# Rounds of seven products in a fused attention and expert kernel: the order of copies, leaky steps, weight splits and decodes

## The chip, the cores and the metric

One core of a Trainium2 chip runs the whole program. The metric is the device time of one execution in microseconds (us), lower is better. Engines are named as the profile names them: PE is TensorE (PEld its weight loads), DVE is VectorE, ACT is ScalarE, POOL is GpSimd, SP is SyncE, which here issues the weight loads. Each engine works through its own queue in order, and a step that waits holds up all that stands behind it in that queue.

## The reference

Causal attention over 2 x 12 heads of 448 positions and 64 dims gives a matrix x of 896 tokens by 768. Two expert layers follow:

```python
h = x @ w_in                      # 768 -> 2048, the part that this change is about
g = np.maximum(0.01 * h, h)       # "leaky"
x = g @ w_out                     # 2048 -> 768
xn = x / rms(x) * rms_g
y = (silu(xn @ w_gate) * (xn @ w_val)) @ w_out2
```

The inputs arrive as 64-bit floats in HBM, the output is 32-bit.

## The kernel before, in words

**Stages.** Attention takes the first 92 us of the profiled execution, `x @ w_in` the stretch from 92 to 204 us, `g @ w_out` runs to 325 us, the gated layer and the last product fill the rest. All matrix work is done with each 32-bit operand split in a high part and a low part, so a product of one 128-row block of weights takes three matmuls: high by high, low by high, high by low.

**Decoding a piece of weights** (`decode`, L96 to L145). A piece n is 128 x 768 values of 64 bits. Its steps are: `load` (SP issues the transfer into one of two `raw` buffers), `rebias` on ACT (L112, writes tile `we`, called e(n) here), `last` on DVE (L119, `ws`), `shift` on DVE (L123) and `sign` on DVE (L127), which finish e(n), then `high` on ACT (L134) and `low` on DVE (L140), which split e(n). `begin(n)` does the load, `word(n)` does rebias to sign, `act(n)` the high and `dve(n)` the low part. The tile `we` has two buffers, so e(n) takes the place of e(n-2), and rebias(n) waits until e(n-2) was read for the last time.

**Straight blocks.** The 2048 outputs are 16 blocks of 128. Blocks 0 to 7 are computed plainly: `block(f)` is 36 matmuls on piece f, and `leaky` on ACT (L214) writes the result to its place. Between them the operand x is prepared for what comes later: `whole_x(c)` (DVE, L601), `xsums(c)` (DVE, L605 to L608), `xsplit(c, 0)` (two copies on ACT, L565) and `xsplit(c, 1)` (two subtractions on DVE, L148), for c of 0, 1, 2.

**Rounds of seven products.** Blocks 8 to 15 are taken in pairs, n of 4 to 7 (blocks f = 2n and f + 1), by Winograd's form of Strassen's scheme: seven products of 9 matmuls each in place of eight. The weights of a round are the quarters a11, a12 (from e(2n)) and a21, a22 (from e(2n+1)). `combine(n)` makes their four sums on POOL (L587) into the tiles `suma` and `sumb`. `plain(n)` splits a11 and a12 (products 1 and 2), `corner(n)` splits a22 (product 4, tiles `hid` and `lod`), `sums(n, 0)` splits `suma` (products 6 and 7), `sums(n, 1)` splits `sumb` (products 5 and 3, tiles `hie` and `loe`). Each split is a copy on ACT (L565) and a subtraction on DVE (L148).

**Order in a round** on PE: 6, 7, 5, then 1 of the next round, 3, 2 of the next round, 4. Products 1, 6, 5 and 3 add to one PSUM bank, one after the other, and each partial sum has to be copied out by ACT (`held`, L627) before the next product adds to the bank: call these copies t1 (after 1), u2 (after 6) and u4 (after 5). Products 7 and 4 share a second bank, and 2 has a third. `join` (DVE, L631) adds a kept copy and a bank, `bend` (ACT, L214) is leaky on a joined block. So product 5 waits for u2, product 3 for u4, the next round's product 6 for t1, and product 4 for the join that reads the second bank. Before, the queue of ACT in a round is: copies of `plain(n+1)`, `bend(f-1, 0)`, copy of `corner(n+1)`, u2, u4, copy of `sums(n+1, 0)`, t1, rebias(f+4), `bend(f+1, 1)`, rebias(f+5), copy of `sums(n+1, 1)`, `leaky(f, 1)`, `bend(f+2, 0)`.

**What sets the order.** Up to the end of the rounds the instructions stand on each engine as the text writes them (`manual_schedule`, L544). From L795 on a planner in the framework orders them by what is ready, and it can move them forward: the first steps of the next stage, `turn_in` (L799 to L804: a copy on ACT, L802, and a subtraction on DVE, L148, that split a block of g), run in the trace among the steps of the last round. In the next stage the first matmuls need `turn_in` of the first blocks and the split pieces 16 and 17.

Of the kernel before, what the change touches and what calls it, by code (L numbers as in the profile page):

```python
# [15 lines left out]
P = 128  # L16
# [58 lines left out]
def fused_kernel(tc, q, k, v, w_in, w_out, w_gate, w_val, w_out2, rms_g, out):  # L75
# [3 lines left out]
    with ExitStack() as top:  # L79
# [13 lines left out]

        xT = [slot(f"a{i}") for i in range(KC)]

        def decode(src, n, m, hi=None, lo=None):  # L96


            N = n * m
            L = {}  # L100

            def load(_=None):
                raw = wst.tile([P, N], I64, tag="raw", name="raw")
                SP.dma_start(out=raw.rearrange("p (n m) -> p n m", m=m), in_=src)
                L["w"] = raw.bitcast(I32).rearrange("p (n t) -> p n t", t=2)

            def rebias(eng="A"):

                e = L["e"] = wst.tile([P, N], I32, tag="we", name="we")[:]
                out, src = e.bitcast(F32), L["w"][:, :, 1].bitcast(F32)  # L110
                if eng == "A":
                    ACT.activation(out=out, in_=src, func=AF.Copy, scale=2.0 ** -112)  # L112
                else:
                    POOL.tensor_scalar(out=out, in0=src, scalar1=2.0 ** -112, scalar2=1.0, op0=ALU.mult, op1=ALU.mult)

            def last(_=None):

                s = L["s"] = wst.tile([P, N], I32, tag="ws", name="ws", bufs=1)[:]
                DVE.tensor_scalar(out=s, in0=L["w"][:, :, 0].bitcast(U32), scalar1=2.0 ** -29, scalar2=7.0,  # L119
                                  op0=ALU.mult, op1=ALU.min)  # L120

            def shift(_=None):
                DVE.scalar_tensor_tensor(out=L["e"], in0=L["e"], scalar=3, in1=L["s"],  # L123
                                         op0=ALU.logical_shift_left, op1=ALU.bitwise_or)

            def sign(_=None):
                DVE.scalar_tensor_tensor(out=L["e"], in0=L["w"][:, :, 1], scalar=-0x80000000, in1=L["e"],  # L127
                                         op0=ALU.bitwise_and, op1=ALU.bitwise_or)

            def high(eng="A"):  # L130
                L["hi"] = wst.tile([P, N], F32R, tag="hi", name="hi") if hi is None else hi
                L["lo"] = wst.tile([P, N], F32R, tag="lo", name="lo") if lo is None else lo
                if eng == "A":
                    ACT.copy(out=L["hi"], in_=L["e"].bitcast(F32))  # L134
                else:
                    POOL.tensor_scalar(out=L["hi"], in0=L["e"].bitcast(F32), scalar1=1.0, scalar2=1.0,
                                       op0=ALU.mult, op1=ALU.mult)

            def low(_=None):
                DVE.tensor_tensor(out=L["lo"], in0=L["e"].bitcast(F32), in1=L["hi"].bitcast(F32), op=ALU.subtract)  # L140

            def parts():
                return [(L["hi"][:, i * m:(i + 1) * m], L["lo"][:, i * m:(i + 1) * m]) for i in range(n)]

            return [load, rebias, last, shift, sign, high, low], parts, L  # L145
# [398 lines left out]
        with tc.manual_schedule(), tc.tile_pool(name="w1", bufs=1) as w1:  # L544
            enc, steps_of, aw, xs, ub, parts_at = {}, {}, {}, {}, {}, {}

            def begin(n):
                src, k_, m_, _ = pieces[n]
                steps_of[n], parts_at[n], enc[n] = decode(src, k_, m_)
                steps_of[n][0]()  # L550

            def run(n, lo, hi):
# [6 lines left out]
            def place(pool, tag, n, bufs=None):  # L559
                kw = {} if bufs is None else dict(bufs=bufs)  # L560
                return [pool.tile([P, n], F32R, tag=t, name=t, **kw) for t in ("hi" + tag, "lo" + tag)]

            def split(pair, x, what=2):
                if what != 1:
                    ACT.copy(out=pair[0], in_=x)  # L565
                if what:
                    rest(pair[1], x, pair[0])

            def e(n, j):
                return enc[2 * n + j]["e"].bitcast(F32)  # L570

            def plain(n):
                pair = place(wst, "", 2 * THIRD)
                split(pair, e(n, 0))
                aw[n, 1], aw[n, 2] = halves(*pair)

            def corner(n):
                aw[n, 4] = place(w1, "d", THIRD, 2)
                split(aw[n, 4], e(n, 1)[:, THIRD:])

            def combine(n):
# [21 lines left out]
            def xsums(c):  # L603
                x = xs[c]
                DVE.tensor_tensor(out=x[:, 0].rearrange("p (b s) -> p b s", b=B), in0=x[:, :, S:],  # L605
                                  in1=x[:, 0].rearrange("p (b s) -> p b s", b=B), op=ALU.subtract)
                DVE.tensor_tensor(out=x[:, 1, S:], in0=x[:, 1, S:], in1=x[:, 0, :S], op=ALU.subtract)
                DVE.tensor_tensor(out=x[:, 1, :S], in0=x[:, 1, :S], in1=x[:, 1, S:], op=ALU.subtract)  # L608

            def xsplit(c, what):  # L610
                for i in (1, 0):
                    t = xs[c, i] = slot(SUMS[c][i]) if what == 0 else xs[c, i]
                    split((t[:, 0], t[:, 1]), xs[c][:, i], what)
                    for b, m in enumerate(((5, 7), (4, 6))[i]):
                        xs[c, "p", m] = cols(t, b)
                xs[c, "p", 1], xs[c, "p", 2], xs[c, "p", 3] = cols(xT[c], 0), cols(xT[c + 3], 0), cols(xT[c + 3], 1)
# [16 lines left out]
            def bend(f, b):  # L633
                leaky(f, b, kept(f, b))
# [21 lines left out]
            def word(n):  # L656
                run(n, 1, 5)

            def bent(f, pss):
                for b in range(B):  # L660
                    leaky(f, b, pss[b])
# [20 lines left out]
            dve(3)  # L682
            leaky(1, 1, ps)
            xsplit(0, 1)
            xsums(1)
            xsplit(1, 0)
            word(4)
            begin(5)
            pss = block(2)
            act(4)  # L690
            xsplit(1, 1)
            dve(4)
            bent(2, pss)
            word(5)
            begin(6)
            pss = block(3)
            act(5)
            whole_x(2)
            dve(5)
            bent(3, pss)  # L700
            xsums(2)
            xsplit(2, 0)
            word(6)
# [17 lines left out]
            combine(4)  # L721
            pss = block(6)
            plain(4)
            corner(4)
            bent(6, pss)
            sums(4, 1)
            pss = block(7)
            sums(4, 0)
            bent(7, pss)
            gF.append(slot(HOME[4], F32))  # L730
            word(10)
# [3 lines left out]
            begin(13)  # L735
            two(4)
            join(8, 0, ub[4, 1], ub[4, "b"])
            bend(8, 0)
            combine(5)
            for n in range(4, LAST + 1):  # L740
                more = n < LAST
                f = 2 * n
                if more:
                    plain(n + 1)
                    if n > 4:
                        bend(f - 1, 0)
                    corner(n + 1)
                else:
                    bend(f - 1, 0)
                times(n, 6, ub[n], start=False)  # L750
                u2 = held(mx, "t0", ub[n])
                v_ = bank()
                times(n, 7, v_)
                times(n, 5, ub[n], start=False)
                u4 = held(mx, "t2", ub[n])
                join(f + 1, 1, u4, v_)
                if more:
                    sums(n + 1, 0)
                    one_(n + 1)
                    word(f + 4)  # L760
                    if f + 6 < NF1 + 2:
                        begin(f + 6)
                    bend(f + 1, 1)
                    run(f + 5, 1, 2)
                else:
                    two(n)
                    bend(f + 1, 1)
                    act(NF1)
                    dve(NF1)
                times(n, 3, ub[n], start=False)  # L770
                if more:
                    sums(n + 1, 1)
                leaky(f, 1, ub[n])
                if more:
                    run(f + 5, 2, 5)
                    if f + 7 < NF1 + 2:
                        begin(f + 7)
                    gF.append(slot(HOME[n + 1], F32))
                else:
                    act(NF1 + 1)  # L780
                    dve(NF1 + 1)
                if n + 1 < LAST:
                    two(n + 1)
                    join(f + 2, 0, ub[n + 1, 1], ub[n + 1, "b"])
                    bend(f + 2, 0)
                elif not more:
                    join(f, 0, ub[n, 1], ub[n, "b"])
                    bend(f, 0)
                if n + 2 <= LAST:
                    combine(n + 2)  # L790
                times(n, 4, v_, start=False)
                join(f + 1, 0, u2, v_)
# [157 lines left out]
```

## Time and profile before

| what | value |
|---|---|
| runs, us | 591.24, 591.34 (median), 591.89 |
| the profiled execution's own time, us | 589.87 |
| its span, first to last instruction, us | 588.1 |
| granted TensorE clock, mean | 1.00 of full speed |
| PE busy | 576.2 us, 98% of the span, 3246 matmuls |
| DVE, ACT, POOL busy | 417.8, 282.0, 75.9 us |
| transfers | 65.02 MB, mean 111 GB/s |

PE's busy share is near its end, so what can be saved without removing matmuls is PE's idle time. Idle time of another engine counts only where PE ends up waiting for it. The profiled execution was 1.47 us (0.25%) shorter than the median of the three runs.

### The profile page before, as it was taken

The numbers are of one execution on the slowest core, as the hardware profiler recorded it, in microseconds if no ns is written. First come the engines' busy times: TensorE is split into PE (matmuls) and PEld (weight loads), VectorE is DVE, ScalarE is ACT, GpSimd is POOL, SyncE is SP. The second block draws the span as 40 slices with busy tenths as digits, with TensorE's granted clock in tenths as the row PEclk, the third lists the DMA queues.
The fourth block names the chain that finished last, engine by engine and source line by source line (L and its number), as shares of the span: only waits on it lengthen the run. The fifth ranks groups of instructions, "written<-read, shape, count | busy, mean of one in ns | idle before, by whom it ended". The sixth has DMA issues, their size and how long they took to land.

```text
span 588.1 us, 8475 instructions
## 1 busy us (share of the span) xinstructions
PE 576.2 (98%) x3246; PEld 520.1 (88%) x3246; DVE 417.8 (71%) x728; ACT 282.0 (48%) x537; POOL 75.9 (13%) x137
## 2 busy tenths in 40 slices
PE   9999999999799999999999999999999999999997
PEld 6687778889688899999999999999999999999997
DVE  6989878886777895765755998797797796840000
ACT  6999984344555682432334743443443444420000
POOL 6666650003333000000000000000000000000000
PEclk9999999999999999999999999999999999999999
DMA  8974403135333323253234244343343351721001
GB/s 182 204 188 81 131 1 108 53 109 161 108 107 108 107 72 107 91 177 110 90 107 124 94 159 152 116 153 116 108 159 111 108 159 56 192 76 41 27 28 40
DMA packets 83351, 65.02 MB, mean 111 GB/s; under 512 B 35440, under 2 KB 80240, under 8 KB 83312
## 3 DMA queue, kind: packets, MB, share of 16 engines
q1 hardware_dynamic: 82352, 64.27, 37.3%
q8 instruction: 25, 0.41, 0.3%
q10 hardware_dynamic: 960, 0.23, 0.2%
q14 instruction: 14, 0.11, 0.1%
HBM read 61.74 MB, written 2.75 MB: 110 GB/s over the span
## 4 chain that ended last, share of the span: by engine, by line
PE 82%; issue 10%; ACT 4%; DVE 3%; POOL 1%; POOLq 0%; ACTq 0%; DVEq 0%
PE mm L154 10%; PE mm L155 10%; PE mm L153 10%; PE mm L824 7%; PE mm L823 7%; PE mm L822 7%; PE mm L907 5%; PE mm L905 5%; PE mm L906 5%; PE pt L386 4%; PE x L408 3%; PE mm L623 3%; PE s L347 3%; PE qk L292 2%; ACT we L112 1%
## 5 line engine op out<-in xcount | busy, mean ns | idle before, releaser
L154 PE MATMUL mm<-a,lo 128*128 128x448 f32 x324 | 118.5, 366 | 0.8 <-DVE lo L140 0.8
L153 PE MATMUL mm<-a,hi 128*128 128x448 f32 x324 | 118.5, 366 | 0.0
L155 PE MATMUL mm<-a,hi 128*128 128x448 f32 x324 | 118.3, 365 | 0.0
L123 DVE SCALAR_TENSOR_TENSOR we<-we,ws 128x768 int32<-128x768 int32 (+1 forms) x70 | 65.5, 936 | 29.0 <-ACT we L112 27.5
L134 ACT CAST hi<-we 128x768 fp32r<-128x768 f32 (+1 forms) x51 | 41.4, 812 | 87.4 <-PE mm L823 38.9
L112 ACT ACTIVATE we<-raw 128x768 f32<-128x768 f32 (+1 forms) x68 | 60.3, 889 | 36.1 <-DVE lo L140 19.2
L140 DVE TENSOR_TENSOR lo<-we,hi 128x768 fp32r<-128x768 f32 (+1 forms) x52 | 47.9, 923 | 26.8 <-ACT hi L134 26.7
L154 PEld LDWEIGHTS mm<-a,lo 128*128 128x128 f32 x324 | 60.9, 188 | 6.3 <-DVE lo L140 1.5
L127 DVE SCALAR_TENSOR_TENSOR we<-raw,we 128x768 int32<-128x768 int32 (+1 forms) x70 | 65.1, 931 | 1.3
L153 PEld LDWEIGHTS mm<-a,hi 128*128 128x128 f32 x324 | 60.9, 188 | 4.8
L155 PEld LDWEIGHTS mm<-a,hi 128*128 128x128 f32 x324 | 60.9, 188 | 4.8
L823 PE MATMUL mm<-b,hi 128*128 128x448 f32 x156 | 57.0, 365 | 0.0
L822 PE MATMUL mm<-b,hi 128*128 128x448 f32 x156 | 57.0, 365 | 0.0
L824 PE MATMUL mm<-b,lo 128*128 128x448 f32 x156 | 56.7, 365 | 0.0
L366 ACT ACTIVATE p<-p,st 128x128 f32<-128x128 f32 (+3 forms) x84 | 44.3, 539 | 1.0 <-DVE st L357 1.0
L119 DVE TENSOR_SCALAR ws<-raw 128x768 int32<-128x768 uint32 (+1 forms) x70 | 38.3, 547 | 7.0 <-DMA raw<-in_moe_w_out_dram 6.0
L379 POOL TENSOR_SCALAR p<-p,st 128x384 f32<-128x384 f32 (+3 forms) x78 | 40.0, 529 | 10.6 <-DVE st L375 7.5
L918 DVE COPY o<-mm 128x384 f32<-128x384 f32 x6 | 3.3, 555 | 53.1 <-PE mm L907 53.1
L916 ACT COPY o<-mm 128x384 f32<-128x384 f32 x8 | 3.8, 478 | 61.8 <-PE mm L907 61.8
L823 PEld LDWEIGHTS mm<-b,hi 128*128 128x128 f32 x156 | 29.3, 188 | 2.3
L824 PEld LDWEIGHTS mm<-b,lo 128*128 128x128 f32 x156 | 29.3, 188 | 2.3
L822 PEld LDWEIGHTS mm<-b,hi 128*128 128x128 f32 x156 | 29.3, 188 | 2.3
(196 smaller groups left out, 1150.8 us busy)
## 6 DMA issues: line engine op xcount, KB each, us to landing
raw<-in_moe_w_out_dram SPq DMA_DIRECT2D x24, 768.0 KB, 4.3
raw<-in_moe_w_in_dram SPq DMA_DIRECT2D x16, 768.0 KB, 4.7
raw<-in_moe_w_gate_dram SPq DMA_DIRECT2D x12, 768.0 KB, 4.4
raw<-in_moe_w_val_dram SPq DMA_DIRECT2D x12, 768.0 KB, 4.4
raw<-in_moe_w_out_dram SPq DMA_DIRECT2D x6, 512.0 KB, 3.5
out_dram<-o SPq DMA_DIRECT2D x14, 192.0 KB, 1.9
n<-in_k_dram SPq DMA_DIRECT2D x22, 112.0 KB, 3.2
n<-in_q_dram SPq DMA_DIRECT2D x22, 112.0 KB, 3.5
```

Source lines behind the costliest of these rows:

```text
L112: ACT.activation(out=out, in_=src, func=AF.Copy, scale=2.0 ** -112)
L123: DVE.scalar_tensor_tensor(out=L["e"], in0=L["e"], scalar=3, in1=L["s"], op0=ALU.logical_shift_left, op1=ALU.bitwise_or)
L127: DVE.scalar_tensor_tensor(out=L["e"], in0=L["w"][:, :, 1], scalar=-0x80000000, in1=L["e"], op0=ALU.bitwise_and, op1=ALU.bitwise_or)
L134: ACT.copy(out=L["hi"], in_=L["e"].bitcast(F32))
L140: DVE.tensor_tensor(out=L["lo"], in0=L["e"].bitcast(F32), in1=L["hi"].bitcast(F32), op=ALU.subtract)
L153: PE.matmul(ps, wh, ah, start=(i == 0), stop=False)
L154: PE.matmul(ps, wl, ah, start=False, stop=False)
L155: PE.matmul(ps, wh, al, start=False, stop=(i == n - 1))
L366: ACT.activation(out=pr, in_=pr, func=AF.Exp, scale=-1.0, bias=st[:, 0, m:m + 1], accum_out=st[:, 1, m:m + 1])
L822: PE.matmul(pss[m, b], wh, ah, start=(f == 0), stop=False)
L823: PE.matmul(pss[m, b], wh, al, start=False, stop=False)
L824: PE.matmul(pss[m, b], wl, ah, start=False, stop=(f == NF1 - 1))
```

## The change

The diff is complete. In the prologue it moves `xsums(1)`, `xsplit(1, 0)`, `xsplit(1, 1)` and `whole_x(2)` behind other steps, swaps the two `sums` of round 4 and takes `corner(4)` out. In the rounds it issues u2 right behind product 6, and behind it the splits of `plain(n+1)`, the `bend`s that the round before left, and `corner(n)`, which was made a round earlier and had two buffers. `word(f+4)` moves forward by two products and `word(f+5)` stays whole. `sums(n+1, 1)` has its ACT copy ahead of `leaky(f, 1)` and its DVE part behind. Pieces 10, 13 and 16 get a third buffer for `we`, so that from piece 11 on e(n) takes the place of e(n-3).

```diff
--- before.py
+++ after.py
@@ -93,7 +93,7 @@
 
         xT = [slot(f"a{i}") for i in range(KC)]
 
-        def decode(src, n, m, hi=None, lo=None):
+        def decode(src, n, m, hi=None, lo=None, room=None):
 
 
             N = n * m
@@ -106,7 +106,7 @@
 
             def rebias(eng="A"):
 
-                e = L["e"] = wst.tile([P, N], I32, tag="we", name="we")[:]
+                e = L["e"] = (room or wst).tile([P, N], I32, tag="we", name="we")[:]
                 out, src = e.bitcast(F32), L["w"][:, :, 1].bitcast(F32)
                 if eng == "A":
                     ACT.activation(out=out, in_=src, func=AF.Copy, scale=2.0 ** -112)
@@ -546,7 +546,7 @@
 
             def begin(n):
                 src, k_, m_, _ = pieces[n]
-                steps_of[n], parts_at[n], enc[n] = decode(src, k_, m_)
+                steps_of[n], parts_at[n], enc[n] = decode(src, k_, m_, room=w1 if n >= 8 and n % 3 == 1 else None)
                 steps_of[n][0]()
 
             def run(n, lo, hi):
@@ -569,13 +569,13 @@
             def e(n, j):
                 return enc[2 * n + j]["e"].bitcast(F32)
 
-            def plain(n):
-                pair = place(wst, "", 2 * THIRD)
-                split(pair, e(n, 0))
+            def plain(n, what=2):
+                pair = aw[n, "p"] = place(wst, "", 2 * THIRD) if what != 1 else aw[n, "p"]
+                split(pair, e(n, 0), what)
                 aw[n, 1], aw[n, 2] = halves(*pair)
 
             def corner(n):
-                aw[n, 4] = place(w1, "d", THIRD, 2)
+                aw[n, 4] = place(w1, "d", THIRD)
                 split(aw[n, 4], e(n, 1)[:, THIRD:])
 
             def combine(n):
@@ -682,22 +682,22 @@
             dve(3)
             leaky(1, 1, ps)
             xsplit(0, 1)
-            xsums(1)
-            xsplit(1, 0)
             word(4)
             begin(5)
             pss = block(2)
             act(4)
-            xsplit(1, 1)
+            xsums(1)
             dve(4)
             bent(2, pss)
+            xsplit(1, 0)
             word(5)
             begin(6)
+            xsplit(1, 1)
             pss = block(3)
             act(5)
-            whole_x(2)
             dve(5)
             bent(3, pss)
+            whole_x(2)
             xsums(2)
             xsplit(2, 0)
             word(6)
@@ -721,11 +721,10 @@
             combine(4)
             pss = block(6)
             plain(4)
-            corner(4)
             bent(6, pss)
-            sums(4, 1)
             pss = block(7)
             sums(4, 0)
+            sums(4, 1)
             bent(7, pss)
             gF.append(slot(HOME[4], F32))
             word(10)
@@ -735,20 +734,26 @@
             begin(13)
             two(4)
             join(8, 0, ub[4, 1], ub[4, "b"])
-            bend(8, 0)
             combine(5)
+            bends = [(8, 0)]
             for n in range(4, LAST + 1):
                 more = n < LAST
                 f = 2 * n
-                if more:
-                    plain(n + 1)
-                    if n > 4:
-                        bend(f - 1, 0)
-                    corner(n + 1)
-                else:
-                    bend(f - 1, 0)
+                if more and n > 4:
+                    plain(n + 1, 0)
                 times(n, 6, ub[n], start=False)
                 u2 = held(mx, "t0", ub[n])
+                if more:
+                    if n == 4:
+                        plain(n + 1, 0)
+                    plain(n + 1, 1)
+                for at in bends:
+                    bend(*at)
+                corner(n)
+                if more:
+                    word(f + 4)
+                    if f + 6 < NF1 + 2:
+                        begin(f + 6)
                 v_ = bank()
                 times(n, 7, v_)
                 times(n, 5, ub[n], start=False)
@@ -757,11 +762,10 @@
                 if more:
                     sums(n + 1, 0)
                     one_(n + 1)
-                    word(f + 4)
-                    if f + 6 < NF1 + 2:
-                        begin(f + 6)
                     bend(f + 1, 1)
-                    run(f + 5, 1, 2)
+                    word(f + 5)
+                    if f + 7 < NF1 + 2:
+                        begin(f + 7)
                 else:
                     two(n)
                     bend(f + 1, 1)
@@ -769,20 +773,19 @@
                     dve(NF1)
                 times(n, 3, ub[n], start=False)
                 if more:
-                    sums(n + 1, 1)
+                    sums(n + 1, 1, 0)
                 leaky(f, 1, ub[n])
                 if more:
-                    run(f + 5, 2, 5)
-                    if f + 7 < NF1 + 2:
-                        begin(f + 7)
+                    sums(n + 1, 1, 1)
                     gF.append(slot(HOME[n + 1], F32))
                 else:
                     act(NF1 + 1)
                     dve(NF1 + 1)
+                bends = [(f + 1, 0)]
                 if n + 1 < LAST:
                     two(n + 1)
                     join(f + 2, 0, ub[n + 1, 1], ub[n + 1, "b"])
-                    bend(f + 2, 0)
+                    bends = [(f + 2, 0), (f + 1, 0)]
                 elif not more:
                     join(f, 0, ub[n, 1], ub[n, "b"])
                     bend(f, 0)
```

## Rows read from the trace of the kernel before

**Rows 1.** Busy time by stretch: length, PE, PEld, DVE, ACT, POOL, clock, DMA
```profile
145.00:204.00 59.00, 52.34 (x254) 46.89 (x253) 44.67 (x54) 34.25 (x57) 15.31 (x13) 1.00 0.34 107
204.00:325.00 121.00, 121.00 (x598) 111.86 (x597) 83.18 (x115) 52.71 (x78) 0.00 (x0) 1.00 0.34 111
```

**Rows 2.** Waits of PE, whole span: us in total, times, longest
```profile
PE mm L623 <- ACT held L627: 6.7, 5, 2.9
PE mm L154 <- DVE lo L140: 0.8, 2, 0.5
```

**Rows 3.** Timeline of PE where it waits: start, us, line, tiles, [idle before <-releaser]
```profile
115.44 0.47 PE L154 MATMUL mm<-a,lo 128*128 128x448 f32 x1 [0.46 <-DVE lo L140]
...
130.62 0.47 PE L154 MATMUL mm<-a,lo 128*128 128x448 f32 x1 [0.32 <-DVE lo L140]
...
149.69 0.47 PE L623 MATMUL mm<-b,hi 128*128 128x448 f32 x1 [0.77 <-ACT held L627]
...
156.48 0.47 PE L623 MATMUL mm<-a,hie 128*128 128x448 f32 x1 [2.88 <-ACT held L627]
...
169.16 0.36 PE L623 MATMUL mm<-b,hi 128*128 128x448 f32 x1
170.45 0.47 PE L623 MATMUL mm<-a,hie 128*128 128x448 f32 x1 [0.93 <-ACT held L627]
170.76 0.37 PE L623 MATMUL mm<-a,loe 128*128 128x448 f32 x1
...
196.77 0.47 PE L623 MATMUL mm<-a,hie 128*128 128x448 f32 x1 [1.14 <-ACT held L627]
```

**Rows 4.** Timeline of ACT in round five, up to the copy u2
```profile
167.79 0.58 ACT L214 ACTIVATE b<-b 128x448 f32<-128x448 f32 x1 [3.57 <-DVE b L631]
...
169.47 0.50 ACT L565 CAST hid<-we 128x384 fp32r<-128x384 f32 x1
169.88 0.52 ACT L627 COPY held<-mm 128x448 f32<-128x448 f32 x1
```

**Rows 5.** Timelines of ACT and of DVE between blocks two and four
```profile
107.95 1.78 ACT L565 CAST b<-b 128x896 fp32r<-128x896 f32 x2 [4.77 <-DVE b L608]
...
110.56 0.96 DVE L123 SCALAR_TENSOR_TENSOR we<-we,ws 128x768 int32<-128x768 int32 x1 [2.18 <-ACT we L112]
...
114.44 0.95 DVE L140 TENSOR_TENSOR lo<-we,hi 128x768 fp32r<-128x768 f32 x1
```

**Rows 6.** Timelines around the start of round four
```profile
141.03 1.44 POOL L587 TENSOR_TENSOR suma<-we 128x384 f32<-128x384 f32 x1 [55.31 <-issue]
...
149.09 0.55 ACT L627 COPY held<-mm 128x448 f32<-128x448 f32 x1
...
154.29 0.58 ACT L214 ACTIVATE b<-b 128x448 f32<-128x448 f32 x1 [3.85 <-DVE b L631]
...
153.65 0.61 DVE L631 TENSOR_TENSOR b<-held,mm 128x448 f32<-128x448 f32 x1
```

**Rows 7.** Timelines of DVE and POOL, side by side and apart
```profile
159.91 0.96 DVE L148 TENSOR_TENSOR lo<-suma,hi 128x768 fp32r<-128x768 f32 x1
...
169.12 1.08 DVE L148 TENSOR_TENSOR lo<-we,hi 128x768 fp32r<-128x768 f32 x1 [0.84 <-ACT hi L565]
170.13 1.36 DVE L148 TENSOR_TENSOR lod<-we,hid 128x384 fp32r<-128x384 f32 x1
...
153.90 0.99 POOL L587 TENSOR_TENSOR suma<-we 128x384 f32<-128x384 f32 x1 [7.96 <-DVE we L127]
...
169.47 1.60 POOL L587 TENSOR_TENSOR suma<-sumb,we 128x384 f32<-128x384 f32 x1
```

**Rows 8.** Transfers issued: KB each, median us to landing
```profile
raw<-in_moe_w_in_dram SPq DMA_DIRECT2D x16, 768.0 KB, 4.7
```

**Rows 9.** Timelines of ACT and DVE at the end of round seven
```profile
197.68 0.94 ACT L802 CAST a<-a 128x896 fp32r<-128x896 f32 x1 [0.96 <-PE mm L623]
...
203.20 1.88 DVE L140 TENSOR_TENSOR lo<-we,hi 128x768 fp32r<-128x768 f32 x2
```

## The prediction

> **What bounds the kernel now.** I read four views in this order. Busy time by stretch says where PE is not at its end: between 145 and 204 us, the rounds of seven products, PE is busy 52.34 of 59 us, while from 204 to 325 us it is busy throughout; the granted clock is 1.00 in both, so a stall costs its own length and no slower matmuls behind it [rows 1]. The list of PE's waits names what is to be had: 6.7 us in five waits for the copies of partial sums, 0.8 us in two waits for the low part of a decoded piece [rows 2]. PE's timeline shows the seven places [rows 3]. Matmuls follow each other by 0.203 us, so after the one at 169.16 the next was due at 169.36; it came at 170.45, and its successor 0.31 behind it. That is 1.20 us lost where the listed idle time is 0.93: a wait costs its idle time and 0.27 more. The seven waits thus cost 0.73 and 0.59 (before blocks four and six), 1.03 (product 6 of round four, behind t1), 3.15 (product 5 of round four, behind u2), 1.20 twice (product 5 of rounds five and six; one of the two is shown) and 1.41 (product 5 of round seven): 9.3 us, the most that any reordering here can bring. Last, ACT's timeline says why the copies are late. In round five u2 starts at 169.88, though product 6 gave its sum about 2.2 us earlier (the nine matmuls of product 7 that end near 169.4 came behind it): in front of it stand a bend that made ACT idle for 3.57 us, waiting for a join on DVE, then three more steps, the corner's copy the last [rows 4].
>
> **Straight blocks.** Before, `xsums(1)` and the two copies of `xsplit(1, 0)` (from 107.95) stand ahead of rebias(4), so DVE idles 2.18 us until shift(4) at 110.56, and the low part of piece 4, 0.95 us from 114.44, comes too late for block four [rows 5]. Now word(4) goes first: rebias(4) is ready when DVE comes to shift(4), and the low part is done near 111.3, over 3 us before block four wants it. The first stall, 0.73, goes. The same idle time then turns up ahead of shift(5), behind the same two copies, but DVE now has the low part of piece 4 to do in it; DVE's whole chain up to the low part of piece 6 gets shorter by about 0.85 (bounds: 0.73, one stall gone and nothing else, to 0.95). PE arrives at block six 0.73 earlier and the low part 0.85 earlier: that stall stays, at 0.47 in place of 0.59. **Gain 0.85.** The decode of pieces 7 to 9 follows from there, transfers included, so all up to round four shifts by as much.
>
> **Into round four.** t1 ran at 149.09, behind the split of `sumb`, which waits for POOL, then two leaky steps and rebias(10). Now the copy of `suma`, some 0.75 us, is taken before that wait and not after it. Without the corner's low part beside it POOL's first sum should also take less than 1.44 [rows 6], near the 0.99 that it takes apart [rows 7]. Both together are worth 0.75 to 1.6 us, the stall is 1.03: I take all of it, as only the lower bound leaves some 0.3. **Gain 1.03.**
>
> **Round four.** Let product 6 start at 0; products end at 1.83, 3.65, 5.48 (product 5), 7.30 (product 1), and product 3 is due at 7.30. u2 runs at 2.03 to 2.5, and product 5 at 3.65 no longer waits: 3.15 goes. What is late next is u4. Ahead of it on ACT now stand the copy of `plain(5)`, `bend(8, 0)`, the corner's copy and rebias(12). The bend waits for its join, which before ran 3.96 after product 6's start [rows 3, 6]; the decode chain in front of it is the same, only product 6 starts a little later against it, so I take 3.6. The join takes 0.61, the bend 0.58: corner's copy from 4.7 to 5.2. Rebias(12) writes the buffer of e(9), so it waits until the corner's low part on DVE has read it. DVE and POOL hinder each other. Beside POOL a low part of 768 columns takes 1.08 where it takes 0.96 apart, one of 384 columns 1.36, POOL's sum 1.60 where it takes 0.99, and the ends fit together as if one always waits for the other: the 384 columns end 0.42 behind POOL's end at 171.07 [rows 7]. `combine(5)` starts at about 3.85 here, so by that reading: POOL's first sum to 4.84, low part of `plain(5)` to 5.64, second sum to 6.50, corner's low part to 6.93, rebias(12) to 7.85, u4 from 7.76 to 8.28, product 3 at 8.34 in place of 7.30. With 0.11 for the restart that is a new stall of 1.15. Bounds: none, if the corner's low part runs unhindered (done at 5.7; the raw piece lands 4.7 after sign(10) let it go [rows 8], at 5.9; u4 ends at 7.25), and 2.0, if a third sum goes ahead of it. I take 1.15, since the rows always show POOL beside this step. **Gain 2.00.**
>
> The Trainium skill ("SBUF — State Buffer", section "SBUF: two separate sides") speaks against this place for the corner: a DVE instruction with two SBUF inputs and a GpSimd instruction share one port pair, and whichever starts first holds it to its end. Were 1.36 instead the step's own price with no port in it, the new stall would be 0.75 and the total 0.4 us better; the rows fit the page's rule, POOL's 1.60 above all.
>
> **Rounds five to seven.** u2 now stands behind the copy of `plain(n+1)` alone, whose source is long ready and whose buffer came free with product 2. It runs at 2.03 to 2.5, product 5 is due at 3.65: 1.15 us of cover. Then two bends to 3.4, whose joins end by then, corner's copy to 3.9, its low part to 4.3 alone or 5.25 behind POOL, rebias to at most 6.15, u4 to at most 6.65, product 3 due at 7.30: 0.65 us of cover, the thinnest of the change. Behind u4, t1 has 5 us of cover; the join of the second bank is done near 8.5 at worst, product 4 due at 9.13 in round six, where product 2 is missing, and 10.95 elsewhere. The third `we` buffer is what lets rebias(f+4) go ahead of `combine(n+1)`'s end. SP's queue holds only loads there; each is issued once sign has read the piece that held its buffer, and by the 4.7 us to landing [rows 8] its piece lands some 4 us before it is wanted. Round seven has no decode, and u2 goes straight behind product 6. **Gain 1.20 + 1.20 + 1.41.** The steps moved behind `leaky(f, 1)` cost DVE and ACT nothing new: the counts stay, and both are under 45 of 59 us [rows 1].
>
> **Behind the rounds** PE has no idle time up to 325 us [rows 1], so what PE gains it keeps. The first turn-in waits for product 5 of round seven and starts at 197.68, the low parts of pieces 16 and 17 at 203.20 [rows 9]: both move with PE.
>
> **Sum.** 0.85 + 1.03 + 2.00 + 1.20 + 1.20 + 1.41 = 7.7 us. The profiled execution, 589.87, would become 582.2 (span 588.1 to 580.4). It is 0.25% under the median of the three runs, so on the median, 591.34, I predict 583.6 us.
>
> **The rivals.**
> *No new stall.* The corner's low part slips between POOL's sums: u4 in time, 8.85 us gained, 582.5. Against it: each time the step stands in the rows POOL holds it up. Chance 0.15.
> *The copy u4 becomes the new wait in every round.* If DVE's chain join, low part, corner, rebias runs 1 to 1.2 us longer than I walked it, the cover of 0.65 is gone: 0.5 to 0.8 in rounds five and six and 2.0 in round four, 2.2 us back: 585.8. For it: ACT's queue is strictly in line, with a bend waiting for a join at its head. Chance 0.22.
> *The copy doesn't come earlier.* If the copy of `plain(n+1)`, now ahead of product 6 in the queue, waits for its buffer or source, u2 is late as before in rounds five and six: 2.4 us back, 586.0. Against it: product 2 ended 1.83 us before product 6 begins. Chance 0.05.
> *Slower.* The planner orders what follows L795 anew. DVE is full there. If it lets turn-ins pass the low parts of pieces 16 and 17, PE stands at the start of `g @ w_out`: each of the twelve later turn-ins costs DVE about 1 us, so from eight of them on the gain is spent, and all twelve give 595.6. For it: turn-ins already run ahead of steps that the text has first [rows 9]. Against it: the low parts came in time before, and nothing that they wait for moves against PE. Chance 0.05.
>
> **How the numbers follow.** My forecast has 0.48 (its own range 582.8 to 584.6), the rivals 0.47 as above; 0.05 is left for gains and losses that cancel. About 0.2% (1.2 us) is what a measurement of this kernel can tell from no change. Faster takes the forecast, the first three rivals and a little of the rest: 0.92; within 0.2%: 0.03; slower 0.05. The range goes from the first rival less 0.2%, 581.3, to the second and third plus 0.2%, 587.2.
>
> **What would show it.** PE's waits in the changed kernel: none for u2, one of about 0.9 us of idle time at product 3 of round four behind u4, one of about 0.2 before block six. ACT: copies u2 some 0.2 us behind product 6's last matmul. DVE: the corner's low part near 1.3 us in rounds four to six, near 0.5 in round seven, which has no POOL work. PE starts `g @ w_out` 7.7 us earlier, near 196.4. The prediction is wrong if PE waits over 1 us at product 3 of rounds five or six, or at all behind the rounds.

## The result and the profile after

The changed kernel takes 585.49 us (median of 8 runs, 584.52 to 589.72), the kernel before on the same chips 591.35 (590.22 to 593.12). The ratio is 0.9909, with a 95% interval of 0.9885 to 0.9933: 0.9% faster, clear of zero, and inside the range of the prediction. The likeliest value, 583.6, was 1.9 us too low. The profiled execution took 585.26, its span 583.5 where it was 588.1.

The two stretches that answer to [rows 1] (same columns: length, then PE, PEld, DVE, ACT, POOL, clock, transfers), from the busy time by stretch of the changed kernel:

```profile
145.00:204.00 59.00, 57.43 (x276) 51.27 (x275) 54.25 (x63) 40.20 (x65) 15.88 (x12) 1.00 0.37 116
204.00:325.00 121.00, 120.77 (x595) 111.07 (x594) 81.20 (x112) 50.93 (x75) 0.00 (x0) 1.00 0.33 107
```

PE is busy for 57.43 of 59 us where it was 52.34. DVE and ACT do more in the same 59 us, because the next stage begins in them earlier; in DVE part of it is that steps take longer beside POOL (experiment 4). Behind 204 us a little of PE's time is now lost.

The list of PE's waits, which answers to [rows 2], with three lines left out, one of the warm-up at the start and two of attention:

```profile
PE mm L623 <- ACT held L627: 1.3, 2, 0.8
...
PE mm L154 <- DVE lo L140: 0.3, 1, 0.3
...
PE mm L825 <- ACT hi L134: 0.2, 1, 0.2
PE mm L623 <- DVE lo L148: 0.2, 1, 0.2
```

And PE's timeline at each place where it waits, which answers to [rows 3]; 148.51 has no listed wait, but stands 0.46 behind its neighbour and not 0.21:

```profile
129.77 0.47 PE L154 MATMUL mm<-a,lo 128*128 128x448 f32 x1 [0.32 <-DVE lo L140]
...
148.05 0.37 PE L623 MATMUL mm<-a,hi 128*128 128x448 f32 x1
148.51 0.47 PE L623 MATMUL mm<-b,hi 128*128 128x448 f32 x1
148.82 0.36 PE L623 MATMUL mm<-b,lo 128*128 128x448 f32 x1
...
154.60 0.47 PE L623 MATMUL mm<-a,lo 128*128 128x448 f32 x1 [0.15 <-DVE lo L148]
...
157.24 0.47 PE L623 MATMUL mm<-a,hie 128*128 128x448 f32 x1 [0.76 <-ACT held L627]
...
170.84 0.47 PE L623 MATMUL mm<-a,hie 128*128 128x448 f32 x1 [0.57 <-ACT held L627]
...
214.93 0.47 PE L825 MATMUL mm<-b,hi 128*128 128x448 f32 x1 [0.23 <-ACT hi L134]
```

No product 5 waits for u2 any more. With 0.27 added to a listed idle time, as before, the places cost 0.59 (block six), 0.36 (product 6 of round four, from the starts), 0.42 (product 1 of round four, for the low part of `plain(5)`), 1.03 and 0.84 (product 3 of rounds four and five, behind u4) and 0.50 (the high part of piece 19, in the next stage): 3.7 us where there were 9.3.

ACT's timeline shows u2 where it was put, and what u4 waits behind:

```profile
150.64 0.54 ACT L627 COPY held<-mm 128x448 f32<-128x448 f32 x1 [1.38 <-PE mm L623]
...
155.87 0.90 ACT L112 ACTIVATE we<-raw 128x768 f32<-128x768 f32 x1 [1.78 <-DVE lod L148]
156.67 0.52 ACT L627 COPY held<-mm 128x448 f32<-128x448 f32 x1
...
169.47 0.91 ACT L112 ACTIVATE we<-raw 128x768 f32<-128x768 f32 x1 [2.75 <-POOL sumb L587]
170.27 0.52 ACT L627 COPY held<-mm 128x448 f32<-128x448 f32 x1
```

In round four u2 (150.64) waits for PE alone. Then rebias(12) at 155.87 waits for the corner's low part, and u4 stands behind it; in round five rebias(14) at 169.47 waits for a sum on POOL, and u4 behind that.

**The books of the profiled execution.** The waits that went are worth 9.3 - 3.7 = 5.6 us; attention ended 0.12 earlier by itself (first matmul of the straight blocks at 92.53, before at 92.65). The span fell by 4.6. The rest, 1.1 us, is in no wait. In two stretches, from the wait at 129.77 to the one at 148.51 and from the one at 170.84 to the one at 214.93, matmuls of the same shape follow each other by 0.2067 us on average and not by 0.2027, at a granted clock of 1.00. That is 4.0 ns on each of some 300 matmuls in 61.5 us: 1.2 us. (The kernel before has this spacing for 4 us only, behind 325 us.) PE's timeline has the first matmul of product 4 of round six and the first behind its nine; here they stand 1.86 us apart:

```profile
185.82 0.37 PE L623 MATMUL mm<-b,hid 128*128 128x448 f32 x1
...
187.68 0.37 PE L623 MATMUL mm<-b,hi 128*128 128x448 f32 x1
```

and in a second profile of the same kernel (run 10 below) 1.83:

```profile
185.73 0.37 PE L623 MATMUL mm<-b,hid 128*128 128x448 f32 x1
...
187.56 0.36 PE L623 MATMUL mm<-b,hi 128*128 128x448 f32 x1
```

### The profile page after: what moved, and what is told of

The parts are those of the page before. It is cut to its first block, busy times and chain, and to the rows that moved or that the text cites. A ratio compares the mean times of both kernels' runs of the same rounds, so it can differ in the third digit from the quotient of the medians.

```text
span 583.5 us, 8473 instructions
## 1 busy us (share of the span) xinstructions
PE 576.5 (99%) x3246; PEld 519.5 (89%) x3246; DVE 420.5 (72%) x728; ACT 281.8 (48%) x537; POOL 77.3 (13%) x137
## 4 chain that ended last, share of the span: by engine, by line
PE 88%; DVE 7%; ACT 2%; POOL 1%; issue 1%; DMA 1%; SPq 0%; ACTq 0%; POOLq 0%; DVEq 0%
PE mm L154 11%; PE mm L155 11%; PE mm L153 11%; PE mm L827 7%; PE mm L825 7%; PE mm L826 7%; PE mm L908 5%; PE mm L910 5%; PE mm L909 5%; PE mm L623 5%; PE pt L386 4%; PE x L408 4%; PE s L347 3%; PE qk L292 2%; DVE we L123 1%; DVE we L127 1%
## 5 line engine op out<-in xcount | busy, mean ns | idle before, releaser
L119 DVE TENSOR_SCALAR ws<-raw 128x768 int32<-128x768 uint32 (+1 forms) x70 | 40.4, 577 | 5.7 <-DMA raw<-in_moe_w_out_dram 4.5
```

## The experiments

Eight kernels were run, and run 6 and the changed kernel once more, in three batches, each batch on one chip with the kernel before beside it. Ratios are to the kernel before in the same batch.

**1. The straight blocks alone.** The kernel before with the part of the diff from `xsplit(0, 1)` to `begin(11)`, rounds as before.

> The kernel before with the reordering of the straight blocks alone (xsums, xsplit, whole_x and word(4) up to block five), the rounds as before. Theory: PE's wait before block four goes, the one before block six stays near 0.3 us idle, the five waits for copies stay as they were (6.7 us idle in all), and the first matmul of the rounds comes some 0.85 us earlier than in the kernel before. Rival: the stall only moves, and the rounds start less than 0.3 us earlier.

PE's waits in this run from 92 us on:

```profile
PE mm L623 <- ACT held L627: 6.6, 5, 2.9
PE mm L154 <- DVE lo L140: 0.3, 1, 0.3
```

As the theory has it, one of the two decode waits is gone and the five copies wait as before. From the first matmul of the straight blocks to the awaited one of block six takes 37.24 us here (92.83 to 130.07), 37.24 in the changed kernel and 37.97 before: 0.73 us, the lower bound of the prediction. One run took 590.83. Its profile caught something else. Behind the longest wait the busy time by stretch shows, in the column before the last two, the granted clock:

```profile
150.00:155.50 5.50, 3.20 (x16) 2.63 (x14) 4.00 (x6) 1.64 (x4) 1.95 (x2) 1.00 0.60 169
155.50:158.50 3.00, 2.41 (x7) 2.15 (x8) 2.06 (x2) 0.54 (x2) 2.80 (x2) 0.51 0.65 221
```

and PE's timeline there:

```profile
156.09 0.74 PE L623 MATMUL mm<-a,hie 128*128 128x448 f32 x1 [2.89 <-ACT held L627]
...
157.00 0.57 PE L623 MATMUL mm<-a,hie 128*128 128x448 f32 x1
157.38 0.57 PE L623 MATMUL mm<-b,hie 128*128 128x448 f32 x1
157.75 0.57 PE L623 MATMUL mm<-b,loe 128*128 128x448 f32 x1
```

PE stood still for 2.89 us, and over the 3 us from 155.50, the last 0.6 us of that wait among them, the clock was at 0.51, the lower of its two levels (1.2 GHz) for nearly all of them; the matmuls behind the wait come 0.373 apart in place of 0.203. In the profile of the kernel before, a wait of 2.88 us at the same place left the clock at 1.00. So the wait cost about 1.3 us more in this execution than in that one: 0.23, then six times 0.17 and a rest of 0.05, over the usual restart.

**2. The place of u2 alone.**

```diff
+                times(n, 6, ub[n], start=False)
+                u2 = held(mx, "t0", ub[n])
                 if more:
                     plain(n + 1)
                     if n > 4:
                         bend(f - 1, 0)
                     corner(n + 1)
                 else:
                     bend(f - 1, 0)
-                times(n, 6, ub[n], start=False)
-                u2 = held(mx, "t0", ub[n])
```

> The kernel before with one edit: the copy u2 and product 6 stand ahead of plain(n+1), the bend and corner(n+1). Theory (the place of u2 in the queue of ACT is what counts): the u2 waits of rounds five to seven go (1.20 + 1.20 + 1.41 us), the one of round four shrinks from 3.15 to about 2.0, as bend(8, 0), which waits for its join, still stands ahead of u2 there; t1's 1.03 and the two early stalls stay; 4.9 us gained, 0.8%. Rival (the early decode, the corner in its own round and the third buffer are needed for it): product 3 or product 1 begins to wait in u2's place, and less than 2.5 us is gained.

586.72 us (4 runs), ratio 0.9915 (0.9886 to 0.9945). PE's timeline in its rounds has these waits and no other:

```profile
150.08 0.47 PE L623 MATMUL mm<-b,hi 128*128 128x448 f32 x1 [0.88 <-ACT held L627]
155.74 0.47 PE L623 MATMUL mm<-a,hie 128*128 128x448 f32 x1 [1.75 <-ACT held L627]
158.21 0.47 PE L623 MATMUL mm<-a,lo 128*128 128x448 f32 x1 [0.15 <-DVE lo L148]
```

Rounds five to seven have none, round four's u2 keeps 2.0 us (1.75 and 0.27), as expected; a wait at product 1 of round four (0.15 idle) is new. On the medians 4.98 us were gained where 4.9 were expected, but that they match so closely is luck: the spans of the two profiles differ by 3.7 us (588.1 and 584.4), and the rest is in the median of the kernel before, as shown further down. Two lines moved do most of what the whole change does; the rival, that the early decode and the third buffer are needed for it, falls.

**3. u2 first, and the bend behind it.** As 2, with `bend(f, 0)` taken from where its join stands and put behind `plain(n+1)`.

> As the run with u2 first, and bend(f, 0) stands behind u2 and behind plain(n+1) too; corner a round early, two buffers and the decode as before. Theory: rebias ahead of u4 is what made product 3 wait in the changed kernel, and here rebias stays behind u4; so no product waits for u2 or u4 in any round, t1's 1.03 and the early stalls stay: 7.0 us gained, 1.2%, more than the changed kernel. Rival (the later decode makes the sums late): products 5 or 6 wait for the splits of the sums, and the gain stays under that of the changed kernel, 5.3 us.

584.89 us (4 runs), ratio 0.9887 (0.9856 to 0.9919): at least as good as the changed kernel (584.98 and 585.49 in its two batches), though with the straight blocks, the decode, the corner and the buffers of the kernel before. PE's waits:

```profile
PE mm L623 <- ACT held L627: 1.1, 1, 1.1
PE mm L154 <- DVE lo L140: 0.8, 2, 0.5
...
PE mm L623 <- DVE lo L148: 0.2, 1, 0.2
```

The 1.1 is t1's. No product waits for u2 or u4. Expected were 7.0 us; the medians differ by 6.8, the spans of the profiles by 5.5 (588.1 and 582.6). What the change does beyond these two moves gains 0.73 in the straight blocks and 1.0 at t1 (1.35 lost here, 0.36 there), and gives it back at u4, where it loses 1.87 and this run nothing.

**4. No sums on POOL.** The changed kernel without the four sums of `combine` in rounds five to seven, which split the sums of round four again; so a part of the weights is not the reference's.

```diff
             def combine(n):
+                if n > 4:
+                    aw[n, "t"] = aw[4, "t"]
+                    return
```

> The changed kernel without the weight sums of rounds five to seven on POOL (those rounds split the sums of round four again), so that POOL is idle beside the splits. Theory (DVE waits for POOL to end, instruction by instruction): the corner's low part takes 0.5 us in rounds four to six in place of 1.36, the low part of plain 0.96 in place of 1.56 to 1.69, ws 0.55 in place of 1.37; product 1 no longer waits in round four, product 3 waits 0.2 us or less in round four and not in round five. Rival (the steps have these prices by themselves, by their shape): the durations and the waits at product 3, 0.76 and 0.57 us idle, stay.

One run, 582.19 us. DVE's timeline in round four of the changed kernel, with POOL beside it:

```profile
152.99 1.56 DVE L148 TENSOR_TENSOR lo<-we,hi 128x768 fp32r<-128x768 f32 x1
154.47 1.36 DVE L148 TENSOR_TENSOR lod<-we,hid 128x384 fp32r<-128x384 f32 x1
155.76 1.37 DVE L119 TENSOR_SCALAR ws<-raw 128x768 int32<-128x768 uint32 x1
```

and in this run, with POOL idle:

```profile
152.62 0.95 DVE L148 TENSOR_TENSOR lo<-we,hi 128x768 fp32r<-128x768 f32 x1
153.75 0.56 DVE L148 TENSOR_TENSOR lod<-we,hid 128x384 fp32r<-128x384 f32 x1 [0.18 <-ACT hid L565]
154.30 0.56 DVE L119 TENSOR_SCALAR ws<-raw 128x768 int32<-128x768 uint32 x1
```

The same three instructions take 0.61, 0.80 and 0.81 us less, and DVE is busy for 50.37 us from 145 to 204 us where it was 54.25. The waits at product 1 of round four and at product 3 of round five are gone, and product 3 of round four comes 0.42 behind its neighbour, 0.33 us lost with the restart where it was 1.03. So the length was waiting and not price. The Trainium skill ("SBUF — State Buffer", section "SBUF: two separate sides") has a DVE instruction with two SBUF inputs and a GpSimd instruction that reads SBUF contend for one port pair, which whoever starts first holds to its end. The trace agrees, with 1.36 against 0.56 for the corner's low part.

**5. The third buffer given out by hand.** The description of the change ahead says that from piece 11 on e(n) takes the place of e(n-3). For piece 14 the trace of the changed kernel speaks against it: rebias(14) waits for the last of POOL's sums (169.47 above), which reads piece 12 and not piece 11. So it seems to take the place of piece 12, and 15 that of 11. This run binds the buffers by the number of the piece (the head of `decode` and two more calls that pass the parity are not shown).

```diff
-                e = L["e"] = (room or wst).tile([P, N], I32, tag="we", name="we")[:]
+                e = L["e"] = (room or wst).tile([P, N], I32, tag="wf" if odd and not room else "we", name="we", bufs=1)[:]
...
-                steps_of[n], parts_at[n], enc[n] = decode(src, k_, m_, room=w1 if n >= 8 and n % 3 == 1 else None)
+                steps_of[n], parts_at[n], enc[n] = decode(src, k_, m_, room=w1 if n >= 8 and n % 3 == 1 else None, odd=n % 3 == 0 if n >= 8 else n % 2)
```

> The changed kernel with the three buffers of e(n) given out by hand, so that piece 14 takes the place of piece 11 and not of piece 12 (which combine(6) on POOL still reads), and piece 15 that of 12. Theory: rebias(14) no longer waits for POOL's last sum but for the corner's low part, starts near 168.6 in place of 169.47, and product 3 of round five waits 0.1 us or less in place of 0.57 idle (0.83 lost); round four's waits stay; the time falls by 0.5 to 0.9 us, 0.1%, at the edge of what can be measured. Rival (the wait in round five is DVE's chain behind POOL, not the place of the buffer): product 3 of round five waits as before.

584.90 us (4 runs), ratio 0.9880 (0.9842 to 0.9918); by time alone it can't be told from the changed kernel. The profile can: ACT's timeline has, where the changed kernel had the wait for POOL,

```profile
169.12 0.90 ACT L112 ACTIVATE we<-raw 128x768 f32<-128x768 f32 x1 [1.88 <-DVE lod L148]
169.93 0.52 ACT L627 COPY held<-mm 128x448 f32<-128x448 f32 x1
```

and PE has one wait for a copy, round four's, 0.7 us idle, and none in round five. The place of the buffer was the cause there. The cover was thin even so: product 6 of round five starts at 163.34, so rebias ended 6.7 us behind it, where the prediction had at most 6.15. Rebias came at 169.12 and not at 168.6: all of this run stands 0.5 later from attention on.

**6. The decode behind u4.**

```diff
                 corner(n)
-                if more:
-                    word(f + 4)
-                    if f + 6 < NF1 + 2:
-                        begin(f + 6)
                 v_ = bank()
...
                 join(f + 1, 1, u4, v_)
                 if more:
+                    word(f + 4)
+                    if f + 6 < NF1 + 2:
+                        begin(f + 6)
```

> The changed kernel with one edit: word(f+4) and its load stand behind u4 and the join of the second bank in place of ahead of product 7. Theory (rebias in front of u4, held up by the corner's low part or POOL, is the new wait): no wait at product 3 in any round, u4 some 0.2 us behind product 5's last matmul; 1.85 us less than the changed kernel. Rival (the decode is late then): product 5 or 6 of the next round waits for the split sums, and nothing or less than 0.5 us is gained.

582.20 us (4 runs), ratio 0.9839 (0.9807 to 0.9872); in another batch 582.82 (6 runs), 0.9856 (0.9829 to 0.9882). ACT's timeline in rounds four and five:

```profile
154.06 0.53 ACT L627 COPY held<-mm 128x448 f32<-128x448 f32 x1 [0.21 <-PE mm L623]
155.62 0.91 ACT L112 ACTIVATE we<-raw 128x768 f32<-128x768 f32 x1 [1.03 <-DVE lod L148]
...
167.23 0.54 ACT L627 COPY held<-mm 128x448 f32<-128x448 f32 x1 [1.30 <-PE mm L623]
168.72 0.91 ACT L112 ACTIVATE we<-raw 128x768 f32<-128x768 f32 x1 [0.95 <-POOL sumb L587]
```

Now both u4 copies wait for PE alone, and the two rebias steps still wait, 1.03 for DVE and 0.95 for POOL, but nothing stands behind them that PE needs soon. Product 3 waits in no round. It gained 2.2 to 3.3 us on the changed kernel where 1.85 was expected; its first profile has no stretch of the wider spacing in the rounds, and PE doesn't wait for piece 19 (0.50), which are part of that.

**7 and 8. All waits at once.** Run 7 is run 3 with the straight blocks of the change, the two `sums` of round 4 swapped, `xsplit(2, 1)` behind `word(7)`, t1 and rebias(10) ahead of `bent(7)`, `join(8, 0)` behind `plain(5)` and `bend(f, 0)` behind t1. Run 8 is run 6 with these (the bends as in the change):

```diff
-            xsplit(2, 1)
             pss = block(4)
...
             begin(9)
+            xsplit(2, 1)
...
-            bent(7, pss)
             gF.append(slot(HOME[4], F32))
...
             two(4)
-            join(8, 0, ub[4, 1], ub[4, "b"])
+            bent(7, pss)
             combine(5)
...
                     plain(n + 1, 1)
+                if n == 4:
+                    join(8, 0, ub[4, 1], ub[4, "b"])
                 for at in bends:
```

> The run with u2 first and bends behind it, plus: the reordering of the straight blocks, xsplit(2, 1) behind word(7), t1 ahead of bent(7) with rebias(10) still in front, join(8, 0) behind plain(5), and bend(f, 0) behind t1. Corner, buffers and place of the decode in the rounds as in the kernel before. Theory: none of the seven waits of before is left and none takes its place above 0.2 us idle up to the end of the rounds; 9.0 us less than before, 1.5%, the fastest of all, less what matmuls lose if their spacing goes from 202.7 to 206.7 ns again, which by now I expect only behind a wait of PE or of its weight loads. Rival (something else bounds the rounds, so that a wait moves to the splits of the sums): no better than the run with u2 and the bends, 1.1%.

> The run with the decode behind u4, and the three waits that it has left are taken on as in the run with all edits: xsplit(2, 1) behind word(7), t1 and rebias(10) ahead of bent(7), join(8, 0) behind plain(5). Theory: PE's waits before block six, at product 6 and at product 1 of round four (0.32, 0.18 and 0.14 us idle, 1.4 us lost) go, no wait above 0.2 us comes in their place; up to the end of the rounds 1.2 us or more are gained on the run with the decode behind u4, in the whole 0.5 to 1.4, as the spacing of matmuls may take some of it. Rival (the waits are tied to DVE's chain and turn up one step later): the same time within 0.3 us.

Run 7: 583.94 us (6 runs), ratio 0.9856 (0.9828 to 0.9884). Run 8: 581.57 (5 runs), ratio 0.9827 (0.9804 to 0.9851), the fastest kernel of the study. Neither has a listed wait of PE left from the straight blocks on; the widest gap is at block seven, where a start comes 0.50 behind its neighbour (0.4 us lost). The busy time by stretch of run 8:

```profile
145.00:204.00 59.00, 59.00 (x292) 54.19 (x291) 54.88 (x66) 43.33 (x69) 15.76 (x12) 1.00 0.37 117
204.00:325.00 121.00, 121.00 (x598) 111.84 (x597) 82.48 (x117) 50.84 (x75) 0.00 (x0) 1.00 0.36 113
```

In run 8 PE is busy throughout in both stretches, with the narrow spacing from the straight blocks to the last layer. It gained 1.25 us on run 6 in the same batch, the upper part of what was expected. Run 7, with as few waits, stayed below the 9.0 us expected, 1.5% (8.2 on the medians, 1.4%; 5.8 by the spans of the profiles, 588.1 and 582.3): in its profile the wider spacing stands from 154 to 167 and from 236 to 323 us, 100 us in all, which costs 2.0 us. That also breaks the second half of its expectation: the longer stretch began behind no listed wait, at two starts 0.28 and 0.31 apart, the shorter one at no gap at all.

**9 and 10. Run 6 and the changed kernel again,** for the spacing.

> The run with the decode behind u4 once more, on the same chip as the run above, with five rounds: 582.0 to 583.6 us; the profile shows the same three waits of PE up to the end of the rounds. A stretch with matmuls 206.7 ns apart may stand elsewhere than in its first profile; if it stands at the same places, it belongs to the order of the instructions and not to chance.

> The changed kernel once more, on the same chip: 584.5 to 586.8 us, its waits as in its first profile (block six 0.32, product 6 and 1 of round four 0.2 or less each, product 3 0.76 and 0.57 us idle). The two stretches with matmuls 206.7 ns apart (129 to 148 and 171 to 214 us) stand at the same places if they come from the order of instructions, elsewhere or not at all if by chance; each us of such a stretch costs 0.019 us.

582.82 and 584.98 us (4 runs; ratio 0.9885, 0.9859 to 0.9911). The waits came back, each within 0.06 us. The spacing came back in part: the first profile of run 6 has the wider one for 4 us from 317, the second for 18 us from 130, 24 us from 212 and again 4 us from 318; the changed kernel had it in 61.5 us in its first profile and in some 20 in the second, from 130 to 149 as in the first but not from 171 to 214. So the order of the instructions alone doesn't set it. What does is open.

## Why the prediction was right, and where it was off

The time lies in the range, but outside the forecast's own, 582.8 to 584.6, and next to the 585.8 of the second rival. PE began `g @ w_out` at 198.84, 5.3 us earlier than before (204.17), where 7.7 were predicted.

**The mechanism held.** Of PE's 9.3 us of stalls 7.0 stood behind u2; all of it was predicted to go, and 1.15 to come back behind u4. Every wait for u2 went, u2 runs 0.2 us behind its product, and run 2 shows that its place in ACT's queue alone is worth rounds five to seven and a part of round four. The new wait at product 3 of round four came at 1.03, for the named reason: rebias(12) behind the corner's low part behind POOL (run 4 takes POOL away, and 0.33 of it is left; run 6 takes rebias out of the way, and the wait goes).

**Straight blocks,** 0.85 predicted, 0.73 measured. The stall before block six stayed at 0.59. DVE's shorter chain gained nothing more on it.

**Into round four,** 1.03 predicted, 0.67 measured. The step that failed is that the copy of `suma` is taken ahead of the wait for POOL. It couldn't be: it needs the buffer that block seven reads, and ACT waits for block seven to end. The row of the changed kernel, from ACT's timeline:

```profile
144.79 0.84 ACT L565 CAST hi<-suma 128x768 fp32r<-128x768 f32 x1 [5.20 <-PE mm L155]
```

So behind block seven t1 has two split copies, two leaky steps and rebias(10) ahead of it.

**Round four,** 2.00 predicted, 1.70 measured: 1.03 for u4, and 0.42 at product 1, which the prediction had not on its list. Its own walk put the end of `plain(5)`'s low part at 5.64 with product 1 starting at 5.48 and wanting it one matmul later, a cover of 0.04; POOL's sum took it. The low part took 1.56 us where the walk had 0.8.

**Rounds five to seven,** 3.81 predicted, 2.97 measured. The step that failed is "rebias to at most 6.15", with its cover of 0.65. It was reckoned from the corner's low part, on the ground that each piece takes the place of the one three before. Piece 14 doesn't, and rebias(14) waited for the fourth of POOL's sums (run 5). The walk was too short besides (6.7 in run 5 for 6.15): the low part of `plain(n+1)` took 1.69 beside POOL in rounds five and six. And in round six the corner's low part took 0.64, not the 1.3 that was given as a sign. The rival "u4 becomes the new wait in every round" was thus right for one round of two, for a reason other than the one given.

**Behind the rounds,** 0 predicted, 0.50 lost at the high part of piece 19. By the prediction's own sign, no wait at all behind the rounds, that is a miss. The planner set PE's matmuls there in another order: the first on piece 19 stands ahead of the two on the low part of piece 18 (first row), and in the kernel before behind them (the other rows), where nothing waits.

```profile
215.24 0.56 PE L827 MATMUL mm<-b,lo 128*128 128x448 f32 x2
...
219.58 0.58 PE L824 MATMUL mm<-b,lo 128*128 128x448 f32 x2
220.00 0.36 PE L822 MATMUL mm<-b,hi 128*128 128x448 f32 x1
```

Not on the list either are 1.2 us by spacing of matmuls in that profile: a term that the profile of the kernel before doesn't have, where the spacing is 0.2027 up to 325 us.

The sum on the profiled execution is 4.6 for 7.7. On the medians it is 5.9, because the median of the kernel before contains something that its profile does not. The prediction read from that one profile that a stall brings no slower matmuls behind it; for most runs of the kernel before that is wrong, and the 1.3 us that this added to the gain were not in its sum. That the median came as near to the forecast as it did is luck to that extent. In the three batches of the experiments the kernel before ran 29 times. Ten runs had a mean granted clock of 1.000 and took 589.97 to 590.84 us; the other 19 had 0.994 to 0.999 and took 591.48 to 595.10. Run 1 shows how such a run comes about. The changed kernel, whose longest wait is 0.76 us, had 1.000 in 11 of its 12 runs and 0.999 in one; that one took 589.72, more than its clock accounts for. Of all 46 runs of the kernels that don't have the wait of 2.9 us none is below 0.999, while 18 of the 29 with it are at 0.997 or 0.994. That the clock falls behind that wait is shown in one profile; that it is the cause in the other runs is argued from these clocks.

The rival on the other side, turn-ins ahead of the low parts of pieces 16 and 17, did not happen: no wait stands at the start of `g @ w_out`.

## What to carry to other kernels

Where one engine copies a partial sum out and another waits to add to the same bank, put that copy first behind its product, and look at each of the later copies too: a step placed between two such copies must not itself wait on a third engine. Steps that nobody needs for a long time (leaky steps, the decode of the next round) belong behind the last copy, as run 6 shows with one moved block that added 2 to 3 us to a gain of 6. Read a buffer's place from the program as built and not from the number of buffers: three buffers are no ring when two pools hand them out.

## What the runs showed of the hardware

A wait of PE of 2.88 us left the granted clock at 1.00 in one profile, and one of 2.89 us brought it to 0.51 over 3 us in another, with matmuls 0.373 us apart. A stall near that length can cost its own time or 1.3 us more, from run to run of the same program.

Matmuls of one shape (128 x 448, a new weight tile each) come 0.2027 us apart or 0.2067, for stretches of 4 to 87 us at the same granted clock of 1.00. Some begin behind a wait of PE (130 and 171 us in the changed kernel), others at no gap (212 us in the second profile of run 6, 154 us in run 7); those named here end where two starts stand 0.28 us or more apart. They differ between two runs of the same program. The cause was not found, and no experiment was made for it alone.
